# Second MLP, last chunk: seven products of 256 columns in the second layer, weight sums on GpSimd, two changes of order

## The chip, the cores and the metric

The kernel runs on one core of a Trainium2 chip (trn2). Its metric is the device time in microseconds (us), the median of the runs. The engines are named as in the profile: PE (TensorE; PEld are its loads of the stationary tile), DVE (VectorE), ACT (ScalarE), POOL (GpSimd), SP (SyncE, whose queue issues the DMAs).

## What is computed

In float32, for 4 batches of 576 rows of 512 columns (2304 rows in all, 18 tiles of 128):

```
x = attention(q, k, v)                      # 8 heads of 64, causal window of 128, a slope for each head
h = relu(x^T @ w_tok1) @ w_tok2             # token mixing, 576 -> 256 -> 576
u = x + h^T
u = u + relu(u @ w_ch1) @ w_ch2             # first MLP, 512 -> 1536 -> 512
xn = (u - mean(u)) / sqrt(var(u) + 1e-6) * g
out = u + relu(xn @ wb1) @ wb2              # second MLP, 512 -> 2048 -> 512
```

## The kernel before

Every operand of a matmul is split into a high and a low part (names with h and l: `w1h`, `w1l`), both F32R. A product then is three matmuls: high with high, high with low, low with high. A split is a copy to the high part on ACT and a subtraction on DVE or POOL (`split`, `minus`).

The 18 tiles go through both MLPs in three chunks: 8 tiles (c = 0), 2 tiles (c = 1), 8 tiles (c = 2). `steps` lists (layer, c, tiles, n): a step takes 256 hidden columns (two tiles of 128) through the first layer (`seven_products` for 8 tiles, `two_blocks` for 2) and its ReLU, while the second layer (`second`) of the step before is done. So the second MLP has 8 steps in each chunk, the first MLP 6.

With 8 tiles the first layer is done as a 2x2 scheme of Strassen's kind (Winograd's form): 7 products in place of 8, each of 6 matmuls of 512 columns. Its operands are sums of the blocks of W1 (`w1_of`, per step, into tiles `st`) and of x (`prep_wide`, once per chunk, per half kk of the contraction). The second layer has 8 units, one per tile: 6 matmuls of 512 columns into a PSUM bank (`acc`, two banks in turn), then one addition on DVE into `u`.

The splits of W2 (`w2h`, `w2l`) are made by `w2_of` in chunk c = 0 and written to DRAM; the other chunks load them. `load_w` keeps 6 raw weight tiles `w` ahead; `stage_w` converts further weights from float64 bytes to float32 and puts them into DRAM. `x_tile`, `tok1`, `tok1_end`, `tok2` are the token mixing: split of x, its two products, the ReLU between them.

The order on every engine is made by a planner (`Plan`): each `op` has a cost for the engines on which it may run, and reads and writes. `ranks` gives each an urgency, worked back from the PE operation that needs it (`shift` moves it by so many thousand ns), and `order` runs a list schedule in that order, engine by engine. The program then is fixed: each engine works through its list in order and waits on semaphores. PSUM has 8 banks: `b0` to `b3` for the first layer (of which `b1` and `b3` are kept throughout, `keep`), `p0` and `p1` for transposes, and two for the second layer.

## Time and profile before

| | |
|---|---|
| median of 3 runs | 842.4 us (842.1 to 843.2) |
| profiled execution: its own time | 843.42 us |
| its span, first to last instruction | 841.7 us |
| PE busy | 825.9 us (98%), 4478 matmuls |
| PEld busy | 684.3 us (81%) |
| DVE busy | 624.9 us (74%) |
| ACT busy | 394.7 us (47%) |
| POOL busy | 373.1 us (44%) |

The chain of work that ended last is PE for 88% of the span. The attention and the token mixing take about the first 165 us, the first MLP goes on to about 458 us, and the last chunk of the second MLP begins at 663.43 us. A matmul's listed duration reaches into the next ones, since matmuls are pipelined; its cost in a row of others is the distance of two starts. The two columns that count for an engine are its busy time in a stretch and, in a timeline, what ended its idle time.

### The profile page before, as it was taken

How to read it: one execution, taken by the hardware profiler on the slowest of the kernel's cores; microseconds unless marked ns; L12 is line 12 of the kernel's file. 1: busy time of each engine (PE TensorE's matmuls, PEld its weight loads, DVE VectorE, ACT ScalarE, POOL GpSimd, SP SyncE). 2: the span in 40 equal slices, each digit the busy share in tenths (PEclk: the TensorE clock that was granted, in tenths of full speed). 3: DMA queues.
4: the chain of work that ended last, by engine and by line, in shares of the span. 5: the costliest groups of instructions: out<-in, count | busy, mean ns of one | idle time of the engine just before them, and what ended most of it. 6: DMA issues, size and time to landing. Idle time of an engine off the chain costs nothing.

```text
span 841.7 us, 13438 instructions
## 1 busy us (share of the span) xinstructions
PE 825.9 (98%) x4478; PEld 684.3 (81%) x4478; DVE 624.9 (74%) x1320; ACT 394.7 (47%) x952; POOL 373.1 (44%) x575
## 2 busy tenths in 40 slices
PE   7999999999999999999999999999999999999998
PEld 5777888878888897888887888888889888888886
DVE  5787777987987988987988866878667755555554
ACT  6888776653334544335367223337368222222221
POOL 2785555794423576522347525624244622221110
PEclk9999999999999999999999999999999999999999
DMA  8679745576766899978772432877377762221112
GB/s 295 195 217 243 232 136 180 165 256 213 240 220 216 288 302 344 333 253 274 263 243 76 138 102 55 289 268 237 138 271 246 234 200 76 76 76 50 51 51 100
DMA packets 73700, 164.98 MB, mean 196 GB/s; under 512 B 8352, under 2 KB 8480, under 8 KB 73632
## 3 DMA queue, kind: packets, MB, share of 16 engines
q1 hardware_dynamic: 73152, 162.83, 59.0%
q0 software_dynamic: 480, 1.31, 0.7%
q8 instruction: 35, 0.57, 0.3%
q14 instruction: 33, 0.27, 0.1%
HBM read 131.34 MB, written 31.46 MB: 193 GB/s over the span
## 4 chain that ended last, share of the span: by engine, by line
PE 88%; POOL 3%; DMA 3%; ACT 2%; issue 2%; DVE 1%; SPq 0%; POOLq 0%; ACTq 0%; DVEq 0%
PE acc L1057 13%; PE acc L1059 13%; PE acc L1058 13%; PE b L1001 10%; PE b L999 10%; PE b L1000 10%; PE ps_v L614 3%; PE ps_s L602 2%; PE p L854 2%; PE b L448 1%; PE b L447 1%; PE b L446 1%; DMA v<-v 1%; PE ps_t L659 1%; PE tok L447 1%
## 5 line engine op out<-in xcount | busy, mean ns | idle before, releaser
L1062 DVE TENSOR_TENSOR u<-acc,u 128x512 f32<-128x512 f32 x252 | 173.1, 687 | 69.1 <-PE acc L1059 66.1
L930 ACT ACTIVATE hh<-b 128x512 fp32r<-128x512 f32 (+1 forms) x140 | 74.7, 553 | 266.4 <-PE b L1001 232.6
L1057 PE MATMUL acc<-w2h,hh 128*128 128x512 f32 x504 | 197.7, 392 | 0.8 <-DVE u L1062 0.8
L1059 PE MATMUL acc<-w2h,hl 128*128 128x512 f32 x504 | 196.5, 390 | 0.2 <-DVE hl L932 0.2
L1058 PE MATMUL acc<-w2l,hh 128*128 128x512 f32 x504 | 196.5, 390 | 0.1
L1001 PE MATMUL b<-xh,w1l 128*128 128x512 f32 x392 | 152.9, 390 | 1.3 <-POOL w1l L379 1.2
L1000 PE MATMUL b<-xl,w1h 128*128 128x512 f32 x392 | 152.7, 390 | 0.4 <-DVE xl L377 0.4
L999 PE MATMUL b<-xh,w1h 128*128 128x512 f32 x392 | 152.9, 390 | 0.0
L379 POOL TENSOR_TENSOR w1l<-w,w1h 128x256 fp32r<-128x256 f32 (+1 forms) x96 | 70.6, 758 | 141.8 <-ACT w1h L361 137.6
L932 DVE SCALAR_TENSOR_TENSOR hl<-b,hh 128x512 fp32r<-128x512 f32 (+1 forms) x140 | 85.9, 631 | 59.3 <-ACT hh L930 58.4
L1059 PEld LDWEIGHTS acc<-w2h,hl 128*128 128x128 f32 x504 | 94.6, 188 | 20.8 <-DVE hl L932 0.9
L1057 PEld LDWEIGHTS acc<-w2h,hh 128*128 128x128 f32 x504 | 94.7, 188 | 20.0 <-DVE u L1062 1.2
L1058 PEld LDWEIGHTS acc<-w2l,hh 128*128 128x128 f32 x504 | 94.7, 188 | 19.1 <-DMA w2l<-d207l 0.5
L379 POOL TENSOR_TENSOR w1l<-st,w1h 128x256 fp32r<-128x256 f32 x74 | 58.1, 808 | 99.2 <-ACT w1h L361 93.3
L1001 PEld LDWEIGHTS b<-xh,w1l 128*128 128x128 f32 x392 | 73.6, 188 | 17.8 <-POOL w1l L379 2.6
L1000 PEld LDWEIGHTS b<-xl,w1h 128*128 128x128 f32 x392 | 73.6, 188 | 16.0 <-DVE xl L377 0.8
L999 PEld LDWEIGHTS b<-xh,w1h 128*128 128x128 f32 x392 | 73.6, 188 | 15.6 <-ACT b L361 0.4
L422 ACT ACTIVATE e<-rh 128x512 bf16<-128x512 bf16 (+2 forms) x65 | 41.3, 636 | 67.5 <-DMA rh<-wb 30.3
L652 ACT ACTIVATE pr<-t,mn 128x128 f32<-128x128 f32 x144 | 55.9, 393 | 13.8 <-DVE mn L643 13.7
L377 DVE TENSOR_TENSOR b<-b,p 128x512 f32<-128x512 f32 x56 | 39.0, 696 | 22.4 <-PE b L1001 21.7
L669 POOL TENSOR_SCALAR_AFFINE_SELECT pf<-pf 128x512 f32<-128x512 f32 x64 | 42.3, 661 | 29.5 <-ACT pf L361 27.4
L379 POOL TENSOR_TENSOR st<-w 128x128 f32<-128x128 f32 x76 | 40.1, 553 | 32.5 <-DMA w<-d 20.0
(119 smaller groups left out, 1369.7 us busy)
## 6 DMA issues: line engine op xcount, KB each, us to landing
w<-d SPq DMA_DIRECT2D x88, 256.0 KB, 4.2
rw<-wb SPq DMA_DIRECT2D x32, 512.0 KB, 4.9
rh<-wb SPq DMA_DIRECT2D x32, 512.0 KB, 5.4
rw<-wa SPq DMA_DIRECT2D x24, 512.0 KB, 3.9
rh<-wa SPq DMA_DIRECT2D x24, 512.0 KB, 4.5
d<-y SPq DMA_DIRECT2D x32, 256.0 KB, 4.0
keys<-kT SPq DMA_DIRECT2D x18, 256.0 KB, 4.2
q<-qT SPq DMA_DIRECT2D x18, 256.0 KB, 4.8
```

What stands on the lines that cost most here:

```text
L379: ENGINE[e].tensor_tensor(get()[:, c], ga()[:, c], gb()[:, c], alu)
L652: op({"ACT": 580}, lambda m=m: nc.scalar.activation(out=pr.t[:, m], in_=t.t[:, m], func=AF.Exp, bias=mn.t[:, m:m + 1], scale=-1.0, accum_o ...
L669: op({"POOL": 630}, lambda a=a: nc.gpsimd.affine_select(pf.t[:, a], pf.t[:, 1], [[0, 4], [1 - 2 * a, P]], (ALU.is_ge, ALU.is_gt)[a], 0.0, ...
L930: op({"ACT": act(n, True)}, lambda: nc.scalar.activation(out=hh.t[:, c], in_=go(), func=AF.Relu), [o], [(hh, key)])
L932: mark[0] = op({"DVE": dve(n)}, lambda: nc.vector.scalar_tensor_tensor(out=hl.t[:, c], in0=go(), scalar=0.0, in1=hh.t[:, c].bitcast(F32), ...
L999: nc.tensor.matmul(g.t, wh.t[:, w], xh.t, start=start and k == 0, stop=False, skip_group_check=True)
L1000: nc.tensor.matmul(g.t, wh.t[:, w], xl.t, start=False, stop=False, skip_group_check=True)
L1001: nc.tensor.matmul(g.t, wl.t[:, w], xh.t, start=False, stop=stop and k == 1, skip_group_check=True)
L1057: nc.tensor.matmul(o.t, hh.t[:, c:c + P], wh.t, start=j == 0, stop=False)
L1058: nc.tensor.matmul(o.t, hh.t[:, c:c + P], wl.t, start=False, stop=False)
L1059: nc.tensor.matmul(o.t, hl.t[:, c:c + P], wh.t, start=False, stop=j == 1)
L1062: op({"DVE": dve(DM)}, lambda o=o, i=i: nc.vector.tensor_tensor(u[i].t, o.t, u[i].t, ALU.add), [o], [u[i]])
```

## The change

In the second MLP's last chunk, in all steps but the last, the second layer is done by 7 products of half the columns as well. The 8 tiles are taken as two groups of 2 + 2 tiles; a unit of `second_fast` is one product for one group: 6 matmuls of 256 columns, for two tiles side by side in one bank. `TURNS` gives the order of the 14 units. Bank `a` starts a group's sum and is copied by ACT into a second bank `b` (`fork`, in `p0` or `p1`), in which the sum goes on; `c` is a third. Results are added into `u` by 12 additions, each over half the columns of two tiles, for which `u` becomes one tile.

For this the ReLU's outputs are combined (`parts_of`): s1 = h01 + h11, s3 = h01 - h00, s2 = s1 - h00, s4 = h10 - s2, each split again. The sums of W2's blocks are made in the second MLP's first chunk on POOL (`keep_sums`: 4 differences of 256 columns, 2 splits), written to DRAM as high and low part, and loaded in the last chunk (`sums_of`, into tiles `rw` and `rh` or `y`).

Two changes of the order: at the start of the first MLP, the first step's W1 parts are begun before the last batch's `tok1_end`, the last batch's `tok2` units are given out between the first step's products, and `prep_wide` alternates between its halves; at the start of the second MLP, the sums of W1 for its first step are formed 80 us earlier by rank (`W1_SHIFT`), into the tiles `few`. The attention's last two conversions of weights (`stage_w`, at n = 32 and 34) are left to later ones.

```diff
-X_SHIFT, STAGE_SHIFT = -20, -20
+X_SHIFT, STAGE_SHIFT, W1_SHIFT = -20, -20, -80
...
+FAST2 = ((1, 2),)
+TURNS = [(0, 0), (1, 0), (2, 0), (5, 0), (3, 0), (0, 1), (6, 0), (1, 1), (4, 0), (2, 1), (5, 1), (3, 1), (6, 1), (4, 1)]
...
-    u = [buf("big", [P, DM], F32, f"u{i}") for i in range(NTILE)]
+    u_all = buf("big", [P, NTILE, DM], F32, "u")
+    u = [Part(u_all, lambda t, i=i: t[:, i]) for i in range(NTILE)]
...
-                    if last_of[b] == i2:
+                    if last_of[b] == i2 < NTILE - 1:
...
-                if W_START <= n < 2 * NTILE and (n - W_START) % W_STEP == 0:
+                if W_START <= n < 2 * NTILE - 4 and (n - W_START) % W_STEP == 0:
...
+        if layer == 0 and tiles[0] == 0:
+            return xs, itertools.chain(*zip(pieces(0), pieces(1)))
         return xs, itertools.chain(pieces(0), pieces(1))
...
+        if ahead == "few":
+            pl.shift = W1_SHIFT
+            sums_a()
+            sums_b()
+            pl.shift = 0
+            return lambda: others(*parts())
+        if ahead:
+            early = parts(hidden)
+            return lambda: others(*early)
+        return others(*parts())
...
+    def fast2(s):
+        layer, c, _, n = steps[s]
+        return (layer, c) in FAST2 and n < (NF1, NF2)[layer] // 2 - 1
...
+        if c == 0 and (layer, 2) in FAST2 and n < (NF1, NF2)[layer] // 2 - 1:
+            keep_sums(layer, n, wtiles[used[0] - 2:used[0]], last)
+        return sums_of(layer, n, out) if fast2(s) else out
+
+    def keep_sums(layer, n, w, last):
...
+        sub(0, half(x0, 1), half(x0, 0))
+        sub(1, half(x1, 1), at(0))
+        sub(2, half(x0, 1), half(x1, 1))
+        sub(3, half(x1, 0), at(1))
+        for k in range(2):
...
+            copy(h, gh, f, lambda gf=gf: gf().bitcast(F32), DM, ("ACT",))
+            minus(f, gf, f, lambda gf=gf: gf().bitcast(F32), h, lambda gh=gh: gh().bitcast(F32), DM, ("POOL",))
+            for p, z, gz in (("h", [h], gh), ("l", f, gf)):
+                op({"DMA": 728}, lambda k=k, p=p, gz=gz: nc.sync.dma_start(
+                    out=d[p].t[:, k * DM:(k + 1) * DM], in_=gz().bitcast(F32)), z, [(d[p], k)], last)
...
+    def parts_of(hid, j, half, g):
...
+        if j == half:
+            relu_both("11" if j else "00", True)
+        elif half:
+            h = few()
+            s1 = relu_with("s1", "11", ALU.add)
+            relu_with("s3", "00", ALU.subtract)
+            s2, a = temp("s2"), temps["00"]
+            minus(s2, lambda: s2.t, s1, lambda: s1.t, a, lambda: a.t, CW)
+            split_h("s1", h, 0)
+            split_h("s3", h, 1)
+            split_h("s2", hidden())
+        else:
+            relu_both("01", False)
+            relu_with("s4", "s2", ALU.subtract)
+            split_h("s4", hidden())
...
-            o = buf("psn", [P, DM], F32, "acc", 2)
+            o = buf("pst", [P, DM], F32, "tok", 2)
...
+    def second_fast(s, w2, hid):
...
+            def emit():
+                for p in range(2):
+                    c = slice((2 * g + p) * P, (2 * g + p + 1) * P)
+                    for k, (x, y) in enumerate(((ghh, gwh), (ghh, gwl), (ghl, gwh))):
+                        nc.tensor.matmul(o.t[:, p], x()[:, c], y(), start=start and p == 0 and k == 0,
+                                         stop=stop and p == 1 and k == 2, skip_group_check=True)
+
+            op({"PE": 6 * pe2(HW)}, emit, [hh, hl, wh, wl], [o])
+
+        def fork(group):
+            tag = f"p{group[2]}"
+            a, b = group[3]["a"], buf("psm", [P, 2, HW], F32, tag)
+            group[3]["b"] = b
+            if tag not in clean:
+                clean.add(tag)
+                x = hid["00"][0][0][0]
+                op({"PE": pe(CW)}, lambda: nc.tensor.matmul(
+                    b.t.rearrange("p a b -> p (a b)"), x.t[:, :P], x.t, start=True, stop=False, skip_group_check=True), [x], [b])
+            op({"ACT": act(CW, True)}, lambda: nc.scalar.activation(out=b.t, in_=a.t, func=AF.Copy), [a], [b])
+
+        def add(group, x, other, half):
+            o, i = group[3][x], group[1] if other else group[0]
+            c = slice(half * HW, (half + 1) * HW)
+            op({"DVE": dve(CW)}, lambda: nc.vector.tensor_tensor(
+                u_all.t[:, i:i + 2, c], o.t, u_all.t[:, i:i + 2, c], ALU.add), [o, u[i], u[i + 1]], [u[i], u[i + 1]])
+
+        for k, g in TURNS:
...
+            if k == 0:
+                product(group, "a", "00", "00", True, False)
+                fork(group)
+            elif k == 1:
+                product(group, "c", "s1", "t1", True, False)
+                add(group, "c", True, 1)
+            elif k == 2:
+                product(group, "b", "s2", "t2", False, False)
+                add(group, "b", False, 1)
+            elif k == 3:
+                product(group, "b", "s3", "t3", False, False)
+                add(group, "b", True, 1)
+            elif k == 4:
+                product(group, "b", "11", "t4", False, True)
+                add(group, "b", True, 0)
+            elif k == 5:
+                product(group, "a", "01", "10", False, True)
+                add(group, "a", False, 0)
+            else:
+                product(group, "c", "s4", "11", False, True)
+                add(group, "c", False, 1)
...
+    load_w(W_BUFS)
     for f, *a in rest:
         f(*a)
-    load_w(W_BUFS)
+    begun = w1_of(0, "hidden")
+    tok1_end(B - 1)
...
-        units = second(*before) if before else iter(())
+        units = (second_fast if fast2(before[0]) else second)(*before) if before else (tok2(i) for i in range(NTILE) if batches_of(i)[-1][0] == B - 1)
...
-            parts, ns = seven_products(w1, xs, keep, s == len(steps) - 1, hid), (2, 3, 3, 0)
+            parts = seven_products(w1, xs, keep, s == len(steps) - 1, hid, fast2(s))
+            ns = (6, 8, 0, 0) if before and fast2(before[0]) else (2, 3, 3, 0)
...
+        begun = w1_of(s + 1, "few") if end and c == 2 else None
```

PE, in a step of the last chunk; `acc_9456` is the bank of one unit, `hh`, `hl` the split ReLU outputs. Before, one unit is two products of three matmuls, of 512 columns each:

```order
L1057 MATMUL acc_9456<-w2h_9228,hh_9354 128x512
L1058 MATMUL acc_9456<-w2l_9231,hh_9354 128x512
L1059 MATMUL acc_9456<-w2h_9228,hl_9358 128x512
L1057 MATMUL acc_9456<-w2h_9242,hh_9409 128x512
L1058 MATMUL acc_9456<-w2l_9244,hh_9409 128x512
L1059 MATMUL acc_9456<-w2h_9242,hl_9422 128x512
```

Now three units follow one another before product 3 of the first layer goes on in `b2_9089`: s2 with t2 into the forked bank `p0_9031`, the block 01 with 10 into `tok_9002` (bank a), and s1 with t1 into `tok_9077` (bank c). Of each unit the first of its two tiles is shown:

```order
L1275 MATMUL p0_9031<-rw_8772,hh_9011 128x256
L1275 MATMUL p0_9031<-rh_8792,hh_9011 128x256
L1275 MATMUL p0_9031<-rw_8772,hl_9029 128x256
...
L1275 MATMUL tok_9002<-w2h_8817,hh_9022 128x256
L1275 MATMUL tok_9002<-w2l_8830,hh_9022 128x256
L1275 MATMUL tok_9002<-w2h_8817,hl_9043 128x256
...
L1275 MATMUL tok_9077<-rw_8772,fewh_8971 128x256
L1275 MATMUL tok_9077<-rh_8792,fewh_8971 128x256
L1275 MATMUL tok_9077<-rw_8772,fewl_8981 128x256
...
L1125 MATMUL b2_9089<-xh30_7753,w1h_9054 128x512
```

The units read four kinds of stationary tiles (`hh`, `hl`, `fewh`, `fewl`) and the sums of W2 (`rw`, `rh`), have half the columns, and are 14 in place of 8.

DVE, in the same steps. Before, between two sums into `b3`, the additions into `u` alternate with the splits of the ReLU's output (`hl`) and of W1 (`w1l`):

```order
L1062 TENSOR_TENSOR u12_1669<-acc_9324,u12_1669 128x512
L1062 TENSOR_TENSOR u13_1779<-acc_9332,u13_1779 128x512
L932 SCALAR_TENSOR_TENSOR hl_9358<-b0_9233,hh_9354 128x512
L1062 TENSOR_TENSOR u14_1915<-acc_9347,u14_1915 128x512
L377 TENSOR_TENSOR w1l_9381<-st_9004,w1h_9367 128x512
L1062 TENSOR_TENSOR u15_2050<-acc_9360,u15_2050 128x512
L932 SCALAR_TENSOR_TENSOR hl_9394<-b2_9252,hh_9373 128x512
L932 SCALAR_TENSOR_TENSOR hl_9411<-b3_2598,hh_9407 128x512
L932 SCALAR_TENSOR_TENSOR hl_9422<-b1_2328,hh_9409 128x512
L377 TENSOR_TENSOR w1l_9430<-w_8973,w1h_9424 128x256
L1062 TENSOR_TENSOR u8_1217<-acc_9432,u8_1217 128x512
L1062 TENSOR_TENSOR u9_1299<-acc_9441,u9_1299 128x512
```

Now, from the split of product 6 on, this stands there; ahead of these rows are two `st` (s1 and s3) and three additions into `u`, so that 17 operations follow one another from the end of product 6 to the last row, the addition that frees the bank of `a`:

```order
L1185 SCALAR_TENSOR_TENSOR hl_8991<-b2_8848,hh_8943 128x512
L1294 TENSOR_TENSOR u_324<-p0_8790,u_324 128x2x256
L1190 SCALAR_TENSOR_TENSOR st_9009<-b1_2423,st_8961 128x512
L400 TENSOR_TENSOR st_9024<-w_8417 128x256
L400 TENSOR_TENSOR hl_9029<-st_8961,hh_9011 128x512
L1185 SCALAR_TENSOR_TENSOR hl_9043<-b1_2423,hh_9022 128x512
L1294 TENSOR_TENSOR u_324<-p1_8887,u_324 128x2x256
L1294 TENSOR_TENSOR u_324<-tok_8921,u_324 128x2x256
L400 TENSOR_TENSOR w1l_9073<-st_9024,w1h_9054 128x512
L1294 TENSOR_TENSOR u_324<-p0_9031,u_324 128x2x256
L1294 TENSOR_TENSOR u_324<-tok_9077,u_324 128x2x256
L1294 TENSOR_TENSOR u_324<-tok_9002,u_324 128x2x256
```

There are 12 additions for 8, and between them the sums of ReLU outputs (`st`) and the split of s2 (`hl_9029`).

POOL, in a step of the second MLP's first chunk. Before, it has the low parts of W1 and W2 and the sums of W1 (`st`):

```order
L379 TENSOR_TENSOR w1l_6195<-w_5896,w1h_6182 128x256 x2
L379 TENSOR_TENSOR w1l_6246<-st_5989,w1h_6240 128x256 x2
L379 TENSOR_TENSOR w2l_6277<-w_6210,w2h_6263 128x256 x2
L379 TENSOR_TENSOR st_6329<-w_6291 128x128 x2
L379 TENSOR_TENSOR st_6329<-st_6329,w_6288 128x128 x2
L379 TENSOR_TENSOR w1l_6375<-w_6103,w1h_6362 128x256 x2
```

Now the differences of W2's blocks and their splits (`fewh`) stand among the same kinds of operations, an `x2` or `x4` being that many instructions in a row:

```order
L402 TENSOR_TENSOR w1l_6206<-w_5654,w1h_6190 128x256 x2
L402 TENSOR_TENSOR w1l_6256<-st_5937,w1h_6250 128x256 x2
L402 TENSOR_TENSOR w2l_6286<-w_6226,w2h_6274 128x256 x2
L402 TENSOR_TENSOR fewh_6320<-w_6226 128x128 x2
L402 TENSOR_TENSOR fewh_6320<-w_6226,w_6283 128x128 x2
L402 TENSOR_TENSOR w2l_6341<-w_6283,w2h_6326 128x256 x2
L402 TENSOR_TENSOR fewh_6320<-w_6283,fewh_6320 128x128 x4
L402 TENSOR_TENSOR fewh_6320<-fewh_6320,fewl_6364 128x256 x4
L402 TENSOR_TENSOR w1l_6409<-w_6123,w1h_6393 128x256 x2
```

Between two splits of W1 that PE needs, POOL has 12 more instructions in each of 7 steps.

## Rows read from the trace of the kernel before

**Rows 1.** The page: its head, and PE of part 1.

```profile
span 841.7 us, 13438 instructions
...
PE 825.9 (98%) x4478; PEld 684.3 (81%) x4478; DVE 624.9 (74%) x1320; ACT 394.7 (47%) x952; POOL 373.1 (44%) x575
```

**Rows 2.** Table by stretch: its us, each engine's busy us (instructions).

```profile
190.00:300.00 110.00, 110.00 (x514) 91.85 (x513) 93.15 (x156) 45.98 (x86) 48.76 (x67) 1.00 0.72 237
...
465.00:605.00 140.00, 140.00 (x624) 115.94 (x623) 105.49 (x183) 55.40 (x111) 61.42 (x92) 1.00 0.55 181
680.00:800.00 120.00, 120.00 (x531) 99.38 (x530) 64.59 (x98) 28.06 (x56) 26.29 (x46) 1.00 0.25 81
...
450.00:465.00 15.00, 13.99 (x63) 10.93 (x62) 13.31 (x25) 9.57 (x19) 14.06 (x22) 1.00 0.44 134
```

**Rows 3.** Timeline of PE, one step of the last chunk: start, duration (us).

```profile
700.17 0.39 PE L1057 MATMUL acc<-w2h,hh 128*128 128x512 f32 x1
...
711.05 0.39 PE L1057 MATMUL acc<-w2h,hh 128*128 128x512 f32 x1
```

**Rows 4.** Timeline of PE, matmuls of 256 columns ending chunk 1.

```profile
661.63 0.28 PE L446 MATMUL b<-fewh,w1h 128*128 128x256 f32 x1
...
663.43 0.40 PE L999 MATMUL b<-xh,w1h 128*128 128x512 f32 x1
```

**Rows 5.** Groups, whole span: stationary loads of the second layer.

```profile
L1057 PEld LDWEIGHTS acc<-w2h,hh 128*128 128x128 f32 x504 | 94.7, 188 | 20.0 <-DVE u L1062 1.2
```

**Rows 6.** DVE by form, 680 to 800 us: busy us, mean ns, idle.

```profile
L1062 DVE TENSOR_TENSOR u<-acc,u 128x512 f32<-128x512 f32 x48 | 33.1, 689 | 18.2 <-PE acc L1059 17.6
...
L377 DVE TENSOR_TENSOR w1l<-st,w1h 128x512 fp32r<-128x512 f32 x5 | 6.1, 1215 | 0.0
...
L377 DVE TENSOR_TENSOR st<-w 128x256 f32<-128x256 f32 x4 | 1.8, 442 | 0.0
```

**Rows 7.** Timeline of DVE in a step of the last chunk.

```profile
706.44 1.29 DVE L932 SCALAR_TENSOR_TENSOR hl<-b,hh 128x512 fp32r<-128x512 f32 x2 [3.05 <-ACT hh L930]
...
722.52 0.68 DVE L1062 TENSOR_TENSOR u<-acc,u 128x512 f32<-128x512 f32 x1
723.12 0.68 DVE L932 SCALAR_TENSOR_TENSOR hl<-b,hh 128x512 fp32r<-128x512 f32 x1
```

**Rows 8.** Groups of POOL by form, 465 to 605 us.

```profile
L379 POOL TENSOR_TENSOR w2l<-w,w2h 128x256 fp32r<-128x256 f32 x20 | 16.0, 818 | 20.1 <-ACT w2h L361 19.9
...
L379 POOL TENSOR_TENSOR st<-w 128x128 f32<-128x128 f32 x18 | 9.5, 551 | 2.4 <-DMA w<-d 1.6 <-DVE w L482 0.6
```

**Rows 9.** Groups of ACT, whole span: split from SBUF, bank copy.

```profile
L361 ACT ACTIVATE w1h<-st 128x512 fp32r<-128x512 f32 x56 | 35.2, 629 | 7.5 <-POOL st L379 3.5 <-DVE st L377 3.4 <-PE b L1000 0.7
...
L361 ACT ACTIVATE b<-b 128x512 f32<-128x512 f32 x28 | 16.8, 598 | 2.2 <-PE b L1001 2.1
```

**Rows 10.** Timeline of PE where it waits; in brackets idle us and releaser.

```profile
170.99 0.39 PE L999 MATMUL b<-xh,w1h 128*128 128x512 f32 x1
171.80 0.50 PE L1000 MATMUL b<-xl,w1h 128*128 128x512 f32 x1 [0.41 <-DVE xl L377]
...
172.60 0.40 PE L1000 MATMUL b<-xl,w1h 128*128 128x512 f32 x1
173.36 0.50 PE L1001 MATMUL b<-xh,w1l 128*128 128x512 f32 x1 [0.37 <-POOL w1l L379]
...
329.94 0.39 PE L1000 MATMUL b<-xl,w1h 128*128 128x512 f32 x1
331.15 0.50 PE L1001 MATMUL b<-xh,w1l 128*128 128x512 f32 x1 [0.82 <-POOL w1l L379]
...
456.29 0.39 PE L1059 MATMUL acc<-w2h,hl 128*128 128x512 f32 x1
457.47 0.50 PE L1057 MATMUL acc<-w2h,hh 128*128 128x512 f32 x1 [0.79 <-DVE u L1062]
```

**Rows 11.** DMA queue of SP, whole span: packets, MB, share of 16 engines.

```profile
q1 hardware_dynamic: 73152, 162.83, 59.0%
```

More of the change, by code (lines that the diff above doesn't have):

```diff
@@ L100, in t, with __init__ @@
         return self.tile
+class Part(Buf):
+    def __init__(self, whole, get):
+        self.plan, self.pool, self.spec = whole.plan, whole.pool, whole.spec
+        self.ops, self.track, self.after, self.behind, self.first = [], {}, [], None, set()
+        self.whole, self.get = whole, get
+    @property
+    def t(self):
+        return self.get(self.whole.t)
 class Plan:
@@ L989, in seven_products @@
+    def seven_products(ws, xs, keep, end, hid, fast):
         ba, bb, bc, bd = bank(0), keep[0], bank(2), keep[1]
```

147 lines of the change are left out of this document (123 added, 24 removed).

## The prediction, made before the run

> **What bounds the kernel now.** I read the page first: its head has PE busy for 825.9 of the 841.7 us of the span [rows 1]. A busy PE need not be PE at its peak, so the next view is the table by stretch: in the last chunk of the second MLP (680 to 800 us) PE has no idle time at all while DVE is busy for 64.59 of 120 us, ACT for 28.06 and POOL for 26.29 [rows 2]. Then the timeline of PE gives the pace: 48 products of 512 columns, the number of one step's second layer, take from 700.17 to 711.05, which is 10.88 us or 226.7 ns each, with no gap between two starts [rows 3]. So in this chunk nothing ends a wait of PE; only fewer or shorter matmuls there can shorten it. The granted clock is 1.00 in every stretch of the table, the upper of its two levels (2.4 GHz) [rows 2]. The few waits of PE lie elsewhere, where one stage follows another, and come up with the changes of order below.
>
> **Products of 256 columns: the main term.** `second_fast` replaces, in 7 of the 8 steps of the last chunk, 8 units of 6 matmuls of 512 columns by 14 units (7 products, 2 groups of tiles) of 6 matmuls of 256 columns. The trace of before has matmuls of 256 columns with a new 128x128 stationary tile each, as these will have: in the chunk of two tiles, 15 in a row start between 661.63 and 663.43, 120.0 ns apart [rows 4]. A step's second layer then takes 84 x 0.1200 = 10.08 us in place of 10.88: 0.80 us less, 5.60 us in 7 steps. That is a third of what columns alone would say (an eighth of 10.88 is 1.36 us), since half the columns cost 120.0 and not 113.3 ns. `fork` adds one product of 512 columns for each of two banks, once: 2 x 0.227 = +0.45 us. Net -5.15 us. All else that PE does is the same in number: 7 x 6 matmuls of 512 columns in each first layer.
>
> A stationary load is listed with 188 ns [rows 5], longer than the 120.0 ns from one start to the next, so loads overlap both the matmuls and one another. The Trainium skill (TensorE: Matmul & The Clock Gate, Part 3: Packing small matmuls) says that a weight load overlaps matmuls in flight only when it goes to another group of rows. By that rule this change would be a loss, since it has 84 loads a step for 48; the pace of 120.0 ns speaks against it [rows 4], and I keep the rows. The Trainium skill's same page (Part 2, Back-to-back issue gap) puts the distance of two starts at columns / 2.4 + 2.5 ns, an estimate of 215.8 and 109.2 ns, by which a step would save 10.36 - 9.17 = 1.19 us and the seven 8.3 us in place of 5.6. The rows have 226.7 and 120.0 [rows 3, 4], and the sum goes by these.
>
> **What the other engines get in a fast step** (20.4 us before: 90 x 0.2267; 19.6 after: 9.52 + 10.08).
> DVE: 64.59/120 x 20.4 = 11.0 us now [rows 2]. It gets 12 additions into u for 8 at 689 ns (+2.8), three sums or differences of ReLUs (+2.1), one hl less (-0.7), and one split of 128x512 from SBUF, which the nearest row has at 1215 ns [rows 6] (+1.2): 16.4 of 19.6 us, 84%. Between 190 and 300 us it is busy for 93.15 of 110, 85%, and PE has no idle time there [rows 2], so I take 0 for the load as such. The place where it could matter is a run of 17 operations between the end of product 6 of one step and the start of the unit that reuses the bank of `a` (the second piece of the order). PE has 10 units and 4 products to do meanwhile, 10 x 0.72 + 4 x 1.36 = 12.64 us. By full durations [rows 6] the run is 14 x 0.69 + 0.44 + 2 x 1.215 = 12.5 us, with some 0.5 us for the ends of matmuls (0.28 us long, 0.12 apart) and the hand-overs 13.0: 0.4 us late. But operations that wait for nothing start 0.61 us apart, though each lasts 0.68 (two in 1.29 us, and 722.52 to 723.12) [rows 7]; so counted, it is 14 x 0.61 + 0.40 + 2 x 1.14 + 0.5 = 11.7, and 0.9 us are left. I take 0, and keep 0 to 0.4 us a step.
> POOL: 26.29/120 x 20.4 = 4.5 us, and up to 4 pairs of 128x256 at 2 x 0.82 [rows 8] and some sums of W1: 11 to 14 us of 19.6. ACT: 4.8 us and 8 operations at 0.60 to 0.63 [rows 9]: 9.8. Both have time to spare; their results are wanted 3 to 5 us after they can start. In the first fast step alone the copy of `a` into its second bank stands 6 matmuls (0.72 us) behind its source: 0.16 for the end of the last matmul, 0.60 for the copy [rows 9] and a hand-over are about 0.9. I add 0.2 us, bounds 0 and 0.5.
>
> **The weight sums** are formed while the second MLP's first chunk runs (7 steps of about 20.4 us). POOL gets 8 instructions of 128x128 at 0.55 and 4 of 128x256 at 0.82 a step [rows 8]: 7.7 us, on 61.42/140 x 20.4 = 9.0 [rows 2], 16.7 of 20.4 or 82%. A step's sums are read in the last chunk, eight steps of two tiles and as many of eight later, and only their buffer is wanted by the next step's; what hides them is POOL's idle time. What they cost if that cover is gone: POOL works in order, a pair of them lasts 1.1 or 1.64 us, and behind it stand w1l and w2l, for which PE waits. The trace has such a wait at 331.15: 1.21 us between two starts for 0.23, so 0.98 lost [rows 10]. Bounds 0 and 0.98 a step; I take 0.1 (0.7 in all), as POOL is 94% busy between 450 and 465 us (14.06 of 15) and loses PE 1.0 us in that whole stretch [rows 2]. SP gets four transfers of 256 KB a step in the first chunk and about 1 MB in the last: 59.0% of the engines for 162.83 MB is 3.05 us of share a MB [rows 11], so +0.16 on 0.55 and on 0.25 [rows 2]. These writes stand among the loads of `w` in SP's queue and wait for POOL there; `w` is loaded six tiles ahead, so I put it at nothing.
>
> **The two changes of order.** Into the first MLP PE loses 0.58 us before 171.80 (waiting for an xl of DVE) and 0.53 before 173.36 (a w1l of POOL) [rows 10]. The change begins the first W1 sums and splits ahead of the token mixing's last ReLUs, interleaves the two halves of the preparation, and gives PE the last tok2 products between the first layer's. DVE and POOL have no less to do, so not all of it need go: bounds 0 and 1.1, I take 0.8. Into the second MLP PE loses 0.95 us before 457.47, where the addition into u that frees its bank is late [rows 10]; W1's sums, which stand among DVE's and POOL's operations there, are formed some 80 us of PE time earlier. Bounds 0 and 0.95, I take 0.7. What is late next in both places is an xl, since these stay where they are.
>
> **Sum.** -5.60 + 0.45 + 0.2 + 0.7 - 0.8 - 0.7 = -5.75 us on a span of 841.7: 835.95. The profiled execution itself took 843.42, 1.7 over its span, and the median of the runs is 842.4, 0.7 over that span; on the median's footing the forecast is **836.7 us**.
>
> **Rivals.**
> *The order gives nothing back* (new waits take the place of the old at the two changes of stage, as DVE and POOL have the same work there): 836.7 + 1.5 = 838.2. For it: DVE and POOL are busy for 13.31 and 14.06 of 15 us in the second place.
> *DVE bounds the fast steps*: its run of 17 is late by 0.4 us in each: 836.7 + 2.8 = 839.5, or more if POOL's work beside it lengthens its operations (w1l from SBUF takes 1215 ns, an addition from PSUM 689 [rows 6]). Against it: the overlap of starts.
> *POOL's sums hold up the splits* (the other side): in each of 7 steps a pair stands ahead of a w1l and of a w2l, and PE loses 0.98 us twice: 836.7 - 0.7 + 13.7 = 849.7. It decides from 0.9 us a step on; one such wait a step gives 842.9, no change. Against it: those pairs are wanted late, and POOL keeps 18% idle.
> *Loads of weights are not hidden*: each matmul of 256 columns takes the 188 ns of its load, 84 x 0.188 = 15.8 us a step, 5.7 more than forecast: 836.7 + 40 = 877. The pace of 120.0 ns speaks against it [rows 4]. The Trainium skill's rule on groups of rows, above, would have it so.
> *More than forecast*: both changes of stage lose all their waits, no POOL wait comes, and the one at 331.15 goes in the new order: 836.7 - 0.55 - 0.9 - 0.98 = 834.3. The pace by the Trainium skill's formula, above, would end there too (2.7 us less).
>
> **How the numbers follow.** Forecast 0.50; no gain from order 0.18; DVE 0.14 (0.03 of it beyond 840.7); POOL 0.11 (0.05 near no change, 0.06 slower); loads 0.01; more 0.06. The range from 834.0 to 840.5 leaves out POOL, the loads and the end of DVE's, some 0.16. A difference of 0.2% (1.7 us) is about what a measurement of this kernel can tell from no change. Faster 0.50 + 0.18 + 0.11 + 0.06 = 0.85, same 0.03 + 0.05 = 0.08, slower 0.06 + 0.01 = 0.07.
>
> **What would show it.** Right: in the last chunk matmuls of 256 columns 120 ns apart, a step of 19.6 us in place of 20.4, no idle time of PE; DVE about 80% busy there; POOL about 80% in the second MLP's first chunk, and its w1l and w2l not named as what PE waits for; fewer or shorter waits near 171 and 457 us. Wrong: starts over 125 ns apart; PE waiting on an addition into u from `p` or `tok`, or on w1l, in every fast step; or a step of the first chunk longer than 20.4 us.

## Result and the profile after

The median of the changed kernel is 835.08 us (833.46 to 835.71, 4 runs), that of the kernel before, run beside it, 842.39 (842.10 to 843.20). The ratio is 0.9908, 95% interval 0.9896 to 0.9919: 7.7 us faster (6.8 to 8.8, the ratio's interval taken of 842.39). The forecast was 836.7, its range 834.0 to 840.5. The profiled execution took 835.71 us.

The page of the kernel after: its head, the busy time of each engine, and the queue of SP's transfers. The rows answer to [rows 1, 11].

```profile
span 834.0 us, 14315 instructions
...
PE 820.6 (98%) x4732; PEld 691.7 (83%) x4732; DVE 658.4 (79%) x1372; ACT 430.8 (52%) x1015; POOL 466.4 (56%) x708
...
q1 hardware_dynamic: 79344, 176.98, 63.3%
```

The table by stretch of the kernel after answers to [rows 2]; the last row is the last chunk, which begins earlier now.

```profile
core 0: us, PE busy (x) PEld busy (x) DVE busy (x) ACT busy (x) POOL busy (x), PEclk, DMA share, GB/s
190.00:300.00 110.00, 110.00 (x524) 92.25 (x523) 95.88 (x165) 46.62 (x87) 57.32 (x76) 1.00 0.72 243
450.00:465.00 15.00, 15.00 (x69) 12.31 (x68) 14.83 (x27) 8.54 (x18) 12.88 (x19) 1.00 0.45 150
465.00:605.00 140.00, 139.62 (x617) 114.73 (x617) 112.97 (x188) 62.46 (x121) 93.17 (x143) 1.00 0.71 243
684.00:821.00 137.00, 136.87 (x878) 124.50 (x879) 102.31 (x161) 60.56 (x112) 80.11 (x122) 1.00 0.34 110
```

PE's idle microsecond between 450 and 465 us is gone, and 0.38 us has appeared in the second MLP's first chunk. In the last chunk DVE, POOL and ACT got busier (75%, 58% and 44%), and PE still hardly waits.

The timeline of PE in the kernel after, from the first matmul of one step of the last chunk to that of the next:

```profile
721.26 0.40 PE L1125 MATMUL b<-xh,w1h 128*128 128x512 f32 x1
...
723.36 0.28 PE L1275 MATMUL p<-rw,hh 128*128 128x256 f32 x1
723.48 0.28 PE L1275 MATMUL p<-rh,hh 128*128 128x256 f32 x1
...
740.84 0.40 PE L1125 MATMUL b<-xh,w1h 128*128 128x512 f32 x1
```

Starts stand 120 ns apart, and the step lasts 19.58 us (721.26 to 740.84), as forecast.

**Where the time went.** Three places divide the program: A, the start of the first matmul on the two middle tiles (c = 1) in the first MLP; B, from there to the same place in the second MLP; C, from there to the start of the last matmul. In the timeline of PE of the kernel after these are:

```profile
284.34 0.28 PE L469 MATMUL b<-fewh,w1h 128*128 128x256 f32 x1
...
612.04 0.28 PE L469 MATMUL b<-fewh,w1h 128*128 128x256 f32 x1
...
829.90 0.39 PE L1240 MATMUL tok<-w2h,hl 128*128 128x512 f32 x1
```

So A is 284.34, B 327.70 and C 217.86; read in the same way, the trace before has 284.87, 330.08 and 222.36. Hence 0.5 us came before A, 2.4 in B, 4.5 in C, and 0.3 behind the last matmul. A little work has moved across the first mark: four small transposes of u, behind A in the kernel before, stand ahead of it in every kernel with the first change of order. The timeline of PE, first before, then after:

```profile
266.71 0.60 PE L854 MATMUL p<-ident,u 128*128 128x128 f32 x4
```

```profile
265.74 1.03 PE L878 MATMUL p<-ident,u 128*128 128x128 f32 x8
```

That is 0.4 us, in A with the first change and in B without it (before, halves, old_order, no_first). The table has all kernels of this study, one profiled execution each; the medians and ratios are of many, against the kernel before run beside each.

| kernel | median us | ratio to before, interval | A | B | C |
|---|---|---|---|---|---|
| before | 842.39 | | 284.87 | 330.08 | 222.36 |
| after | 835.08 | 0.9908 (0.9896 to 0.9919) | 284.34 | 327.70 | 217.86 |
| no_fast | 841.13 | 0.9977 (0.9966 to 0.9988) | 286.81 | 326.09 | 222.36 |
| no_fast_held | 840.54 | 0.9971 (0.9959 to 0.9982) | 284.42 | 326.42 | 222.36 |
| sums_only | 844.73 | 1.0015 (1.0004 to 1.0026) | 286.19 | 329.41 | 222.36 |
| old_order | 839.79 | 0.9970 (0.9955 to 0.9984) | 285.04 | 331.02 | 217.86 |
| no_first | 839.72 | 0.9968 (0.9956 to 0.9980) | 284.80 | 329.24 | 217.86 |
| no_few_held | 837.33 | 0.9931 (0.9916 to 0.9947) | 286.06 | 327.60 | 217.88 |
| after_att | 836.11 | 0.9919 (0.9898 to 0.9939) | 286.55 | 327.59 | 217.86 |
| no_sums | 833.63 | 0.9888 (0.9868 to 0.9908) | 283.41 | 326.63 | 217.86 |
| sums_twice | 848.97 | 1.0067 (1.0050 to 1.0085) | 285.91 | 340.11 | 217.85 |
| dve2 | 839.20 | 0.9963 (0.9950 to 0.9976) | 285.05 | 327.11 | 221.18 |
| dve4 | 848.78 | 1.0071 (1.0054 to 1.0087) | 283.39 | 327.14 | 232.46 |
| halves | 849.68 | 1.0078 (1.0063 to 1.0094) | 283.74 | 330.12 | 229.32 |

C repeats to 0.03 us between kernels that share it. B repeats to 0.6 (after, after_att, dve2 and dve4 are issued alike in it). A does not repeat: seven kernels are issued alike up to A, and their traces have 283.39 to 286.06 (after and dve4, no_sums, no_fast_held, dve2, sums_twice, no_few_held). The two latest, sums_twice and no_few_held, are the only two of the seven in which the granted clock fell ahead of A (to between 0.50 and 0.67 from 76 to 80 us). A difference of a microsecond in a median may come from A alone, so prices are read from B and C.

### The profile page after: what moved, and what is told of

Read it like the earlier page. It is cut to its first block, busy times and chain, and to the rows that moved or that the text cites. A ratio compares the mean times of both kernels' runs of the same rounds, so it can differ in the third digit from the quotient of the medians.

```text
span 834.0 us, 14315 instructions
## 1 busy us (share of the span) xinstructions
PE 820.6 (98%) x4732; PEld 691.7 (83%) x4732; DVE 658.4 (79%) x1372; ACT 430.8 (52%) x1015; POOL 466.4 (56%) x708
## 4 chain that ended last, share of the span: by engine, by line
PE 90%; DVE 3%; DMA 3%; ACT 1%; POOL 1%; issue 1%; SPq 0%; ACTq 0%; DVEq 0%; POOLq 0%
PE tok L1238 11%; PE tok L1240 11%; PE tok L1239 10%; PE b L1125 10%; PE b L1126 10%; PE b L1127 10%; PE tok L1275 5%; PE p L1275 4%; PE ps_v L637 3%; PE ps_s L625 2%; PE p L878 2%; PE b L471 2%; PE b L470 2%; PE b L469 2%; PE tok L766 1%; PE tok L764 1%
## 5 line engine op out<-in xcount | busy, mean ns | idle before, releaser
L1243 DVE TENSOR_TENSOR u<-tok,u 128x512 f32<-128x512 f32 x196 | 133.8, 685 | 47.8 <-PE tok L1240 46.1
L1238 PE MATMUL tok<-w2h,hh 128*128 128x512 f32 x392 | 154.2, 393 | 0.2 <-DVE u L1243 0.2
L1240 PE MATMUL tok<-w2h,hl 128*128 128x512 f32 x392 | 153.0, 390 | 0.2 <-DVE hl L958 0.2
L1239 PE MATMUL tok<-w2l,hh 128*128 128x512 f32 x392 | 152.9, 390 | 0.0
L402 POOL TENSOR_TENSOR w1l<-w,w1h 128x256 fp32r<-128x256 f32 (+1 forms) x110 | 77.4, 725 | 103.5 <-ACT w1h L384 99.0
L956 ACT ACTIVATE hh<-b 128x512 fp32r<-128x512 f32 (+1 forms) x112 | 58.7, 542 | 147.1 <-PE b L1127 104.1
L958 DVE SCALAR_TENSOR_TENSOR hl<-b,hh 128x512 fp32r<-128x512 f32 (+1 forms) x112 | 67.4, 617 | 26.3 <-ACT hh L956 25.7
L1240 PEld LDWEIGHTS tok<-w2h,hl 128*128 128x128 f32 x392 | 73.6, 188 | 16.4 <-DVE hl L958 0.8
L1238 PEld LDWEIGHTS tok<-w2h,hh 128*128 128x128 f32 x392 | 73.7, 188 | 15.5 <-DVE u L1243 1.3
L1239 PEld LDWEIGHTS tok<-w2l,hh 128*128 128x128 f32 x392 | 73.7, 188 | 14.3
```

The costliest lines, as they stand in the source:

```text
L402: ENGINE[e].tensor_tensor(get()[:, c], ga()[:, c], gb()[:, c], alu)
L956: op({"ACT": act(n, True)}, lambda: nc.scalar.activation(out=hh.t[:, c], in_=go(), func=AF.Relu), [o], [(hh, key)])
L958: mark[0] = op({"DVE": dve(n)}, lambda: nc.vector.scalar_tensor_tensor(out=hl.t[:, c], in0=go(), scalar=0.0, in1=hh.t[:, c].bitcast(F32), ...
L1238: nc.tensor.matmul(o.t, hh.t[:, c:c + P], wh.t, start=j == 0, stop=False)
L1239: nc.tensor.matmul(o.t, hh.t[:, c:c + P], wl.t, start=False, stop=False)
L1240: nc.tensor.matmul(o.t, hl.t[:, c:c + P], wh.t, start=False, stop=j == 1)
```

## Experiments

**The order alone.** FAST2 is empty: no products of 256 columns in the second layer, no weight sums.

```diff
-FAST2 = ((1, 2),)
+FAST2 = ()
```

> The change without its products of 256 columns and without the weight sums; only the two changes of order stay. My working gave the order 1.5 us: 842.4 - 1.5 = 840.9. The trace after suggests more, 3.0 us (0.5 into the first MLP, 1.0 at its second change of chunk, 1.5 into the second MLP): 839.4. If the order gives nothing back: 842.4, and all of the gain belongs to the last chunk. Between 841.6 and 843.2 speaks for nothing, under 840.2 for more than my terms.

841.13 us, 1.9 less than before (1.0 to 2.9), which fits the 1.5 of the forecast better than the 3.0 that the trace after suggested. A is 2.5 us later than after, and B 4.0 shorter than before. The list of PE's waits has two of 2.2 us together for an addition into u inside the attention, though nothing in the attention was edited. The planner works urgencies back from the program's end, through the rings of buffers that `sums_of` shares with the conversion of weights, so an edit in the last chunk can place the attention's work anew. The longer wait in the timeline of PE:

```profile
90.43 0.79 PE L469 MATMUL tok<-xh,wt1h 128*128 128x512 f32 x1 [1.50 <-DVE u L769]
```

and the table by stretch from there, in which the last column but two is the granted clock:

```profile
90.00:92.00 2.00, 1.57 (x4) 1.18 (x5) 2.00 (x6) 1.14 (x5) 1.14 (x2) 0.61 0.45 153
92.00:94.00 2.00, 2.00 (x11) 1.50 (x11) 0.37 (x1) 1.60 (x7) 0.31 (x1) 0.53 0.40 88
94.00:96.00 2.00, 2.00 (x28) 1.56 (x26) 1.48 (x4) 0.39 (x3) 1.34 (x3) 1.00 1.02 381
```

After the wait PE worked near the lower of its two levels (1.2 GHz) until 94 us.

**The order alone, urgencies held.** To see the edits without that, the urgencies of the kernel after are held for all operations up to the first that differs.

```diff
-FAST2 = ((1, 2),)
+FAST2 = ()
...
+        n = len(RANKS)
+        late[:n] = RANKS
         return late
```

> The order changes alone again, but with the planner's urgencies of the changed kernel held for everything up to the second MLP's first chunk, so that attention and first MLP are issued in its order. Theory: without that, the planner had placed the attention's work anew, and PE waited 2.2 us there for an addition into u; held, the attention ends as in the changed kernel, and what is left apart is the fast products with their sums: 5.15 gained, 0.54 lost in the first fast step, 1.0 in the first chunk. So 835.1 + 3.6 = 838.7. By my recorded terms the fast part is 4.25: 839.3. If the attention's order is not what cost it, it stays at 841.1.

A is 284.42, among those of the order after, and the two waits are gone. Both are in the traces of no_fast and of sums_only (below), which are issued alike up to A, and in none of the seven of the order after: the planner's order was their cause. B and C are 3.2 us above those of after, close to the 3.6 of the theory. The median does not follow: by its interval, 838.9 to 840.9 of 842.39, it leaves out the theory's 838.7 and also the 841.1 of its rival, and its ratio cannot be told from that of no_fast.

**The products alone.** Both changes of order undone, in the lines of the diff that make them. The planner makes a new order from this; it is not that of the kernel before.

```diff
-    begun = w1_of(0, "hidden")
-    tok1_end(B - 1)
...
-        begun = w1_of(s + 1, "few") if end and c == 2 else None
+        begun = None
```

> The products of 256 columns and the weight sums, with both changes of order undone (the new pools stay). By my terms the products, the fork, the first wait and the sums come to -4.25 us: 842.4 - 4.25 = 838.1. If the order gives 3.0 us, this is 835.1 + 3.0 = 838.1 too; if the order gives nothing, it is 835.1. The last chunk's steps last 19.6 us under every theory.

C is 217.86 as after, 4.50 less than before. B is 331.02, 0.9 more than before. PE loses as much by the distance of starts at 536.8 and 581.0 us, where it waits for DVE's hl and u, so this is about the price of the sums in this order. Between 158 and 460 us PE waits again:

```profile
PE tok L764 <- DVE u L769: 1.7, 2, 1.0
PE b L1125 <- POOL w1l L402: 1.1, 1, 1.1
PE tok L1236 <- DVE u L1241: 0.8, 1, 0.8
PE tok L1238 <- DVE hl L956: 0.2, 1, 0.2
```

The same list of the kernel after has no row at all. The waits in the first row are before 175 us, for the token mixing's additions; the kernel before waited there for xl and w1l instead [rows 10]. The median, 839.8, is 1.7 us above the 838.1 of two of the theories; its interval, 838.6 to 841.1 of 842.39, leaves out these as well as the third (835.1).

**One change of order at a time.** Each undone by itself; in the second, urgencies ahead of it are held.

```diff
-                    if last_of[b] == i2 < NTILE - 1:
+                    if last_of[b] == i2:
...
-            return xs, itertools.chain(*zip(pieces(0), pieces(1)))
```

> The changed kernel without its first change of order (token mixing's end, W1 parts, interleaved halves, the two conversions of weights). The waits near 171 to 177 us return (1.4 to 2.2 us) and the attention ends at about 150.3 instead of 152.3 us. The question is the pair of waits at 325.9 and 331.2 us (1.3 us in the kernel before, gone after): theory, this edit moved GpSimd's and VectorE's backlog away and they return: 835.1 + 2.0 - 1.9 + 1.3 = 836.5; rival, they went with the other edits: 835.2.

> The changed kernel without its second change of order (the sums of W1 for the second MLP's first step are formed where they were before), the urgencies of everything ahead of it held. If this edit took away the waits at 451.6 and 457.5 us, they return and the stretch from the first MLP's middle chunk to the second's is 1.3 to 1.7 us longer: 836.6. If the planner's placing of other work took them away, no change: 835.1.

Without the first change the wait on POOL's w1l at the first MLP's last chunk is back, in the timeline of PE of no_first:

```profile
329.53 0.39 PE L1124 MATMUL b<-xl,w1h 128*128 128x512 f32 x1
331.12 0.50 PE L1125 MATMUL b<-xh,w1l 128*128 128x512 f32 x1 [1.20 <-POOL w1l L402]
```

B is 329.24, 1.5 to 2.1 more than in the kernels with that change, and 1.1 to 1.7 more without the four transposes; the wait itself costs 1.36 by the distance of starts. So the theory holds for this wait, and the forecast had left this gain out of its sum. Before 175 us PE waits as well, twice, 1.7 us in all, for the token mixing's additions as in old_order; yet A (284.80) is no later than in the kernels with the change. The median, 839.72, lies 3 us above the 836.5 of the theory, which these waits do not explain. Its own executions spread most: 837.4 to 838.7 at a mean granted clock of 1.000, and 839.2 to 841.7 at 0.995 to 0.998.

Without the second change PE loses 0.36 us near 450 and 0.32 near 455 us, a third of the 0.95 of before in the second place [rows 10]. B, 327.60, lies from 0.1 below to 0.5 above those of after, dve2 and dve4: the change is worth at most 0.5 us here. Its median, 837.33, is nearer to the theory's 836.6 than to 835.1, but three of its five executions ran at a mean granted clock of 0.998, and in the profiled one of these the clock fell ahead of A. With the first change undone the second is worth 331.02 - 329.24 = 1.8 us, or 1.3 without the loss at 581 us, which comes and goes. So the two overlap: most of what the second gives alone the first gives too.

**The attention's order.** Urgencies of the kernel before held for the first 895 operations of the kernel after.

```diff
+        n = len(RANKS)
+        late[:n] = RANKS
         return late
```

> The changed kernel with the urgencies of the kernel before held in the attention (its first 895 operations). The last ps_v starts at 150.6 us in the trace before and at 152.3 in the one after: if the planner's order is the cause, it comes at about 150.5 again and the time is 1.7 less, 833.4. If the difference is one of runs, it stays at 835.1.

The profiled execution does not bear the theory out: the last ps_v starts at 156.09 us, not at 150.5, after a wait of 1.88 us at 16.96 and granted clocks of 0.80, 0.50 and 0.84 in the three stretches of 4 us from 16 on. Three of its executions at clock 1.000 took 833.9 to 834.8 us, three at 0.995 or 0.996 took 837.5 to 837.9. Whether this order is better without such a drop of the clock stays open.

**Sums stored but not used.** `fast2` answers no, `keep_sums` stays.

```diff
-        return (layer, c) in FAST2 and n < (NF1, NF2)[layer] // 2 - 1
+        return False
```

> As the kernel without products of 256 columns, but with the weight sums still formed and stored in the second MLP's first chunk (nothing reads them). My term: +0.7 us against that kernel (0.1 a step). Rival, that a pair of sums holds up a split of W1 or W2 once a step: +6.9 us. Rival, wholly hidden: 0. The trace after shows two waits of 0.3 and 0.4 us in that chunk, both on DVE and none on POOL.

3.6 us more than no_fast, by medians, and 3.3 in B: neither 0 nor 0.7 nor 6.9. PE's large waits in the chunk are three, of 0.58, 0.61 and 1.18 us, on DVE's hl and u, none on POOL. No PE operation wants these sums, so the planner ranks them otherwise than in the kernel after. This prices the sums in another order; the next kernel keeps the order of after.

**The same order without the sums.** POOL issues none of the weight sums, ACT copies raw weights in their place, the transfers and products go on with these. Costs and dependencies given to the planner are the same, so the order is too. The kernel after waits twice in this chunk, by the timeline of PE:

```profile
532.64 0.50 PE L1240 MATMUL tok<-w2h,hl 128*128 128x512 f32 x1 [0.15 <-DVE hl L958]
...
576.96 0.50 PE L1238 MATMUL tok<-w2h,hh 128*128 128x512 f32 x1 [0.23 <-DVE u L1243]
```

```diff
-            minus((x, c), get, *a, *b, HW, ("POOL",))
+            op({"POOL": 2 * pool_tt(HW // 2)}, lambda: None, [a[0], b[0]], [(x, c)])
...
```

> The changed kernel in the same order, with the weight sums left out: GpSimd issues none of them, ScalarE copies the raw weights in their place, and the stores, loads and products go on with these values. Theory A, that GpSimd's work beside it lengthens VectorE's operations from SBUF to SBUF (0.85 and 1.22 us in the trace after, 0.43 and 0.68 in the one without sums): VectorE's busy time between 465 and 605 us falls from 113.0 to about 106, the waits at 532 and 576 us go, 0.7 to 1.1 us less: 834.2. Theory B, that VectorE's order makes these two waits: no change, 835.1. Rival C of the prediction, that a pair of sums holds up a split each step: 7 us less, since such waits would be in the kernel after; its trace names none.

B is 326.63, 0.5 to 1.1 less than in the four traces with the sums in this order (after, after_att, dve2, dve4), and the median 1.5 less than after (intervals 0.9868 to 0.9908 and 0.9896 to 0.9919 overlap). The groups of DVE's instructions between 465 and 605 us, mean ns behind the comma, first of the kernel after:

```profile
L1243 DVE TENSOR_TENSOR u<-tok,u 128x512 f32<-128x512 f32 x54 | 37.0, 686 | 14.4 <-PE tok L1240 13.9
...
L452 DVE TENSOR_SCALAR m<-rw 128x512 uint32<-128x512 uint32 x11 | 7.7, 704 | 0.0
L400 DVE TENSOR_TENSOR w1l<-st,w1h 128x512 fp32r<-128x512 f32 x7 | 6.9, 990 | 0.0
```

and of no_sums:

```profile
L1243 DVE TENSOR_TENSOR u<-tok,u 128x512 f32<-128x512 f32 x54 | 37.0, 688 | 16.3 <-PE tok L1240 15.9
...
L452 DVE TENSOR_SCALAR m<-rw 128x512 uint32<-128x512 uint32 x11 | 5.7, 515 | 0.0
L400 DVE TENSOR_TENSOR w1l<-st,w1h 128x512 fp32r<-128x512 f32 x6 | 5.2, 872 | 0.0
```

Operations that read PSUM last as long as with the sums; most of those from SBUF to SBUF are shorter without POOL's work, and DVE's busy time falls from 112.97 to 108.75 us (theory A had said 106). The timeline of DVE at the wait of 532 us, first after, then no_sums:

```profile
530.54 0.85 DVE L452 TENSOR_SCALAR m<-rw 128x512 uint32<-128x512 uint32 x1
531.31 1.27 DVE L958 SCALAR_TENSOR_TENSOR hl<-b,hh 128x512 fp32r<-128x512 f32 x2
```

```profile
529.43 0.43 DVE L452 TENSOR_SCALAR m<-rw 128x512 uint32<-128x512 uint32 x1
529.78 1.28 DVE L958 SCALAR_TENSOR_TENSOR hl<-b,hh 128x512 fp32r<-128x512 f32 x2
```

The operation ahead of hl takes half as long, DVE is not idle in front of hl in either, and both waits are gone. For the first wait theory A holds: at this matmul PE loses 0.30 to 0.38 us, by the distance of starts, in each of those four traces, and nothing here. The second, at 576 us, is in after and after_att alone: it comes and goes by less than this contention. Theories B (no change) and C (7 us) fall.

**The sums' differences twice.** Same order, each of POOL's four differences issued twice.

```diff
-            minus((x, c), get, *a, *b, HW, ("POOL",))
+            def emit():
+                for _ in range(2):
+                    for q in (slice(0, HW // 2), slice(HW // 2, HW)):
+                        nc.gpsimd.tensor_tensor(get()[:, q], a[1]()[:, q], b[1]()[:, q], ALU.subtract)
...
```

> The changed kernel in the same order, with each of the four differences of the weight sums issued twice: GpSimd gets 8 more instructions a step, 4.2 us, some 119 of 140 us busy between 465 and 605 us. Theory A, contention: VectorE's busy time there goes from 113 to about 117 us and PE's losses in that chunk from 1.06 to about 2 us: 836.1. Rival C, a pair of sums ahead of a split once a step: 7 us more, 842, with w1l and w2l of GpSimd named as what PE waits for.

B grows by 12.4 us, more than either theory (1 and 7). The list of PE's waits between 459 and 628 us has its rows:

```profile
PE b L1132 <- POOL w1l L402: 3.1, 2, 3.0
PE tok L1243 <- ACT hh L956: 2.9, 2, 2.2
PE tok L1243 <- DVE u L1248: 0.9, 1, 0.9
```

The first is rival C. The second is one that nobody had named: the copy of a sum to its high part stands in ACT's queue, waits for POOL, and the ReLU that PE needs stands behind it. The timeline of ACT:

```profile
605.24 0.63 ACT L384 ACTIVATE fewl<-fewh 128x512 fp32r<-128x512 f32 x1 [2.69 <-POOL fewh L1065]
605.77 1.06 ACT L956 ACTIVATE hh<-b 128x512 fp32r<-128x512 f32 x2
```

From 459 us to the end of B ACT waits 35.7 us in all for POOL's sums, in the kernel after 14.6. And the two long waits cost more than themselves, since the granted clock fell behind both; the table by stretch at the first:

```profile
553.00:557.00 4.00, 1.25 (x6) 0.71 (x4) 3.97 (x6) 2.50 (x6) 4.00 (x6) 1.00 0.09 38
557.00:561.00 4.00, 3.79 (x10) 2.99 (x11) 2.89 (x5) 1.06 (x2) 4.00 (x6) 0.57 0.95 280
```

**More work on DVE in the fast steps.** The operation that forms s3 is issued five times (dve4) or three times (dve2), same order.

```diff
-            op({"DVE": dve(CW)}, lambda: nc.vector.scalar_tensor_tensor(
-                out=t.t, in0=g.t, scalar=0.0, in1=z.t, op0=ALU.max, op1=alu), [g, z], [t])
+            def emit():
+                for _ in range(5 if x == "s3" else 1):
+                    i = nc.vector.scalar_tensor_tensor(
+                        out=t.t, in0=g.t, scalar=0.0, in1=z.t, op0=ALU.max, op1=alu)
+                return i
...
```

> The changed kernel in the same order, with the operation that forms s3 issued five times in place of once in each of the seven fast steps: four more operations of 128x512 on VectorE a step. By overlapped starts they take 4 x 0.61 = 2.4 us; my working had 0.9 us to spare, and the trace after has 0.46 more of idle time in that run: 1.05 us late a step, 7.4 in all: 842.5. By full durations (0.69 each, 0.4 late before any is added) 3.2 us a step: 857. If VectorE's load as such is far from the limit (4 x 0.61 on 14.6 of 19.6 us): no change, 835.1.

> As the kernel with four more operations, with two: there the four stood 0.70 us apart, 2.8 in all, and PE waited 1.6 us a step for an addition from a p bank, so 1.2 to 1.3 us were to spare. Two take 1.4: 0.1 to 0.2 late a step, about 1 us in the steps and as much again in the first and the last: 837. If the load of VectorE counts and not the place, half of the four's 13.7: 842.

With four more, PE waits at the same place in five of the seven fast steps, and elsewhere in the first and the last; in its timeline:

```profile
699.60 0.39 PE L1127 MATMUL b<-xh,w1l 128*128 128x512 f32 x1
701.43 0.38 PE L1280 MATMUL p<-rw,hh 128*128 128x256 f32 x1 [1.45 <-DVE u L1299]
```

and DVE has, just before:

```profile
696.59 4.19 DVE L1192 SCALAR_TENSOR_TENSOR st<-b,st 128x512 f32<-128x512 f32 x6 [0.61 <-PE b L1127]
700.70 1.28 DVE L1299 TENSOR_TENSOR u<-p,u 128x512 f32<-128x512 f32 x2
```

Six such operations take 4.19 us for the 1.29 of two in the kernel after: 2.9 more, 0.7 for each, not the 0.61 expected (all of them but the first write the same tile; whether that is why, no run shows). The step is 21.37 us, 1.8 longer than 19.58, so 1.1 us were to spare. With two (2 x 0.7 = 1.4) three steps of four last 19.90 to 19.94: 0.35 longer, again 1.1 to spare. It is the place that counts, not the load: DVE is busy for 75% in the kernel after, and C grows by 3.3 us with two and by 14.6 with four, where a load would give half. The medians, 839.20 and 848.78, each lie between two of the values expected.

**Pace of 256 columns by itself.** The kernel before, with the second layer's matmuls of seven steps cut into halves of 256 columns.

```diff
+                    for m in range(2):
+                        q = slice(m * HW, (m + 1) * HW)
...
+                                nc.tensor.matmul(o.t[:, q], x.t[:, c:c + P], y.t[:, q], start=m + j + k == 0,
```

> The kernel before, with each 512-column matmul of the second layer cut into two of 256 columns in seven steps of the last chunk: the same products, the same additions, twice the matmuls and stationary loads. By the pace of the rows (120.0 for 226.7 ns) 7 x 48 x 13.3 ns = +4.5 us: 846.9. If the starts stood 109.2 and 215.8 ns apart, +0.9 us: 843.3. If each matmul took the 188 ns of its load, 7 x (96 x 0.188 - 10.88) = +50 us: 892.

C grows by 6.96 us (the median by 6.6), 2.5 more than the rows' 4.5. The timeline of PE shows a wait that the cut brings, once a step:

```profile
685.96 0.28 PE L1061 MATMUL acc<-w2l,hh 128*128 128x256 f32 x1
686.30 0.39 PE L1061 MATMUL acc<-w2h,hl 128*128 128x256 f32 x1
...
707.39 0.28 PE L1061 MATMUL acc<-w2l,hh 128*128 128x256 f32 x1
```

and DVE ends the hl that it needs at 684.95 + 1.29 = 686.24:

```profile
684.95 1.29 DVE L932 SCALAR_TENSOR_TENSOR hl<-b,hh 128x512 fp32r<-128x512 f32 x2 [1.30 <-ACT hh L930]
```

With half the columns ahead of it, the matmul on hl comes too early: 0.22 us lost there and 0.10 at the next start. A step is 21.43 us, 1.03 more than the 20.4 before; without the 0.32 it is 0.71, or 14.8 ns for each of 48 pairs, 120.7 ns a matmul. So the pace of [rows 4] is confirmed; the other two times expected, 843.3 and 892 us, are far off.

## Why the prediction was right, point by point

**Products of 256 columns** (-5.60 + 0.45): right. C falls by 4.50 us, and 0.54 of loss in the first fast step (below) stands against it, so 5.04 for 5.15. One remark of the working is wrong, and nothing rests on it: the 0.80 us of a step are three fifths of the 1.36 by columns alone, not a third. The rule of the Trainium skill (TensorE: Matmul & The Clock Gate, Part 3: Packing small matmuls), by which loads to the same rows would not overlap, does not show here: 84 loads a step at 120 ns, none of them awaited.

**The first fast step** (+0.2, the copy of `a`): the step failed in its cause, and the size is 0.54. PE waits for a bank:

```profile
683.47 0.28 PE L1275 MATMUL tok<-w2h,hl 128*128 128x256 f32 x1
684.13 0.36 PE L1275 MATMUL tok<-rw,fewh 128*128 128x256 f32 x1 [0.38 <-DVE u L1243]
```

The bank belongs to the last unit of `second`, whose addition into u stands behind two subtractions on DVE. The copy of `a` is not waited for.

**DVE in a fast step** (0, bounds 0 and 0.4 a step): right, since nothing is lost, and by full durations the run of 17 would have been late. But the place was another. I had 0.9 us to spare in front of the bank of `a`; dve2 and dve4 say 1.1 in front of an addition from `p`. That the two figures are close is luck. The load was 75%, not 84%.

**Weight sums** (+0.7): the size is about right, 0.5 to 1.1 us (no_sums against after, after_att, dve2 and dve4), the mechanism is not. I weighed POOL's queue in front of w1l and w2l; PE loses the time on DVE's hl and u, because DVE's operations from SBUF to SBUF last longer beside POOL's (shown for the wait on hl at 532 us). POOL was 67% busy there, not 82%: the planner gave part of its splits to DVE. Rival C lies closer than 0.11 made it look: some 4 us more of POOL's work a step bring such a wait (2.96 us, once), with ACT's queue as a second way.

**Into the first MLP** (-0.8): the waits are gone as forecast, but whether A is earlier cannot be told: 283.4 to 286.1 in the traces of this order, or 283.0 to 285.6 without the four transposes, against 284.87 and 283.74 in the two of the order before. Part of what was won is lost again in the attention, where PE is busy for 37.05 of the 40 us from 60 on, for 37.79 before. What the change won later I had only as a rival: the wait at 331.15 [rows 10], 1.1 to 1.7 us of B.

**Into the second MLP** (-0.7): the waits are gone. The edit meant for it is worth 1.3 to 1.8 us alone and at most 0.5 beside the first, so the gain belongs to both.

**The sum.** On the span 7.7 us against 5.75. By traces: C -4.50 for -4.95; order in B, -3.7 (before to no_fast_held), or -3.2 without the four transposes, for -0.7; sums +0.5 to +1.1 for +0.7; A -0.5 (-1.0 without the transposes) for -0.8, which its scatter drowns. The undersized term is the order: it removed all of PE's listed waits from A to the second MLP, also the one that I had not put into the sum. The rival *More than forecast* (834.3 us, chance 0.06) had this, all waits of both changes of stage gone and the one at 331.15 too, and but for the price of the sums it describes the outcome better than the forecast. That the forecast is only 1.6 us too high is in part luck.

In medians, order alone (1.9 or 2.4) and products alone (2.5) do not add up to 7.7, though B and C do (3.7 + 3.6 for 6.9). Traces are one execution each: that of before is 1.0 us above its median, that of no_fast_held 1.0 below. All four executions of after ran at a mean granted clock of 1.000, while 5 of 12 of no_fast, 4 of 8 of no_fast_held and 4 of 9 of old_order ran below 0.999. That does not explain no_fast_held, whose executions at 1.000 took 839.5 to 841.1 us, no less than its others (839.3 to 841.0). The rest stays open.

## What to carry to other kernels

Where a planner orders every engine from the program's end, an edit anywhere moves work everywhere; hold the order of what was not edited, or price an edit from stretches of the trace that repeat, before reading a microsecond from a median. Count the work between two marks first: an edit of the order can carry some of it across. A cheap operation put on an idle engine can be paid for on its neighbours: by longer operations on the engine beside it, and by what stands behind its result in another engine's queue. The slack in front of such a place can be measured by repeating one instruction there until PE waits.
